# A DeltaNet and PReLU kernel: the first chunk's two steps in turn, and the first feed-forward product in halves by token

## The chip, the cores and the metric

The kernel runs on one core of a Trainium2 chip. A core has a matrix engine (TensorE, here PE, with its weight loads shown as PEld), VectorE (DVE), ScalarE (ACT), GpSimd (POOL), and SyncE (SP), which here only issues transfers. Each engine works through its own instructions in order, and semaphores tie the engines together. The metric is the device time of one execution in microseconds (us).

## The reference

Two blocks, one behind the other. The first is a DeltaNet recurrence for 4 batches, 8 heads, 768 tokens and head dimension 48; the second is a feed-forward with a learned slope for negative values, for 3072 tokens, model width 384 and inner width 2048.

```python
k_n = k / (norm(k) + 1e-6)
for t in range(768):
    y[:, :, t] = q[:, :, t] @ state
    v_old = state^T @ k_n[:, :, t]
    state = state + beta[:, :, t] * outer(k_n[:, :, t], v[:, :, t] - v_old)
x = y as (batch * token, head * dim)             # 3072 x 384
h = x @ w_in                                     # 384 x 2048
g = maximum(h, 0) + alpha * minimum(h, 0)
out = g @ w_out                                  # 2048 x 384
```

`w_in` and `w_out` arrive as float64 and are turned into float32 on the chip.

## The kernel before

**Steps.** The recurrence is worked in 12 chunks of 64 tokens. A step is one chunk of two of the four batches, so there are 24 steps, numbered so that steps 0 and 1 are chunk 0, steps 2 and 3 chunk 1. Within a step the 64 tokens' dependence on one another is a triangular system. Its two 32-token diagonal blocks are inverted on DVE for four steps together (`eliminate`, `eliminate_small`; a set of four is called m, and `turned` and `inverse` hold the result and its transpose). For the first four steps the inversion is done on 16-token blocks, and small matmuls join the halves: `cross` for steps 2 and 3, and the opening of `first_chunk` for steps 0 and 1. `place` copies the inverse blocks into `inv`; `between_1` and `between_2` compute with PE the block that joins the two 32-token halves (a product, a copy out of PSUM to `mid`, a product, a copy into `inv`). Then `solve` gives the corrected values u, `outputs` the step's y, `next_state` the state behind it, and `to_ffn` turns y round into `xt`, the feed-forward's input, of which a chunk has 256 tokens (128 from each step). For chunk 0 the state is zero, so `through_state` issues nothing. `mask` cuts the query-key products of steps 0 and 1 to the triangle, `scale_v` weights the values.

**Feed-forward.** `ffn_in(c)` computes g for chunk c: 8 pairs of 128 inner columns, each pair 2 x 3 matmuls of 256 tokens into one PSUM bank; ACT (L918) and DVE (L920) then apply the slope. It is a Python generator that yields after each matmul, so other work can be woven in: `alongside(products, pieces)` runs so many matmuls of chunk 0's product and so many parts of weight conversion.

**Weights.** `w_in` comes in 12 pieces of 512 KB (128 rows by 512 columns each, pieces 0 to 2 for the first 512 columns, and so on), each staged in one of six slots that lie in the space of `w_out`. A piece takes two ACT instructions (L225, L226, issued by `begin`) and two parts on DVE (L235, L240; `convert(n)` runs n parts). A slot's next piece is fetched (L209, on SP) when its last one has been converted. `ahead` limits how far ACT may run ahead. `w_out` follows in 16 pieces of 384 KB.

**PSUM.** There are eight banks: three pairs that `ps_big` and `ps_one` hand out in turn, and two for the feed-forward (`ps_ffn`).

**The order by hand.** The engines are scheduled manually: each runs its instructions in the order in which the Python program issues them. After the preparation of steps 0 to 3, `busy(6)` issues products that nothing uses (512 columns each), DVE inverts the 16-token blocks, and `first_chunk` begins. It does each stage for step 0 and step 1 together, with two `busy` products, the 12 parts of conversion of pieces 0 to 5 among and behind the outputs, and the loads for steps 2 to 4 (`load_late`, L161, and `load_v`, L137: 12 transfers in all) between the conversion parts. `second_pair` follows: it works steps 2 and 3 stage by stage, and between the stages runs chunk 0's `ffn_in` (48 matmuls) and 22 parts of conversion. Behind it come chunk 1's `ffn_in`, the next inversion (`eliminate(1)`) and the rest of `w_out`.

Of the kernel before, what the change touches and what calls it, by code (L numbers as in the profile page):

```python
# [28 lines left out]
ALU = mybir.AluOpType  # L29
# [14 lines left out]
def kernel(  # L44
# [36 lines left out]
    def ps_one():  # L81
        return ps_big()[:, 0]
# [494 lines left out]
    def quad(i):  # L577
        return slice(HB * i, HB * i + HB)
# [40 lines left out]

    def place(n, parts=(0, 1, 2, 3), by_vector=False):  # L620
        for _ in placing(n, parts, by_vector):
            pass

    def placing(n, parts, by_vector=False):


        if n >= N:
            return
        m, j = n // NJ, n % NJ
        own = slice(j * H, j * H + H)  # L630

        def put(cols, i):
            out, x = inv[n % NE][:, :, cols], inverse[m][:, own]
            if by_vector:
                nc.vector.tensor_scalar(
                    out=out, in0=x, scalar1=which[:, i : i + 1], scalar2=None, op0=ALU.mult
                )
            else:
                nc.scalar.mul(out, x, which[:, i : i + 1])  # L639

        if 0 in parts and n >= NJ:
            nc.scalar.copy(diag[n % NE], turned[m][:, own])
            yield
        if 1 in parts:
            put(slice(HB, C), 1)
            yield
        if 2 in parts:
            put(slice(0, HB), 0)
            yield
        if 3 in parts:  # L650
            w = stats[n][1]
            for t in range(2):
                nc.scalar.copy(w[half(1 - t), 2], w[half(t), 1])
            yield
# [19 lines left out]

    def copied(n, second, p, vector=False):

        to = inv[n % NE][:, :, HB:C] if second else mid[n % 2]
        to = to.rearrange("p (a g) i -> p a g i", a=2)

        def copies():  # L680
            for t in range(2):
                rows = quad(2 * t + (0 if second else 1))
                if vector:
                    nc.vector.tensor_copy(out=to[rows], in_=p[rows])
                else:
                    nc.scalar.copy(to[rows], p[rows])  # L686

        return [copies]

    def between(*wanted, vector=False):  # L690

        wanted = [
            (n, second, region(p, G * HB, g=G)) for n, second, p in wanted if n < N
        ]
        todo = [products(*x) for x in wanted]
        for i in range(H):
            for product in todo:
                for t in range(2):
                    product(i, t)
        return [y for x in wanted for y in copied(*x, vector)]  # L700

# [8 lines left out]

    def scale_v(n):
        if n < N and n not in nv:
            nv[n] = v_raw.pop(n)
            nc.vector.tensor_tensor(
                out=nv[n], in0=nv[n],
                in1=stats[n][0][:, :, None].to_broadcast([128, H, D]), op=ALU.mult,
            )
# [180 lines left out]

    def ffn_in(c):
        xt = xts[c]  # L900
        gs = gss[c] = []
        later = iter(())
        for f in range(0, FT, 2):
            p_h = ps_ffn().rearrange("p (f i) -> p f i", f=2)
# [23 lines left out]
        for _ in later:  # L928
            pass

    def store(c, u, o_sb):
# [431 lines left out]
    def busy(n, p=None):  # L1363

        p = ps_one() if p is None else p
        while n > 0:
# [7 lines left out]
    def queries():  # L1374
# [17 lines left out]
        return mask  # L1392

    def first_chunk(mask, convert):

        both, bs = (0, 1), 2 * H
        ahead[0] = n_in

        p = ps_one()[:, 0 : bs * LB].rearrange("p (b i) -> p b i", i=LB)
        for b in range(bs):  # L1400
            for i in range(4):
                nc.tensor.matmul(p[quad(i), b], edge[quad(i), b], turned[0][quad(i), b, 0:LB])
        nc.scalar.copy(half_way[:, 0:bs, 0:LB], p)
        begin_in(6)
        busy(0.75)
        one, two = (
            ps_one()[:, 0 : bs * LB].rearrange("p (b i) -> p b i", i=LB) for _ in range(2)
        )
        for b in range(bs):
            for i in (0, 2):  # L1410
                nc.tensor.matmul(
                    one[quad(i), b], inverse[0][quad(i), b], half_way[quad(i), b, 0:LB]
                )
        for i in (0, 2):
            y = turned[0][quad(i), 0:bs, 0:LB]
            nc.vector.tensor_tensor(out=y, in0=y, in1=one[quad(i)], op=ALU.add)
        for b in range(bs):
            for i in range(4):
                nc.tensor.matmul(
                    two[quad(i), b], half_way[quad(i), b], inverse[0][quad(i), b, LB:HB]  # L1420
                )
        scale_v(0)
        y = inverse[0][:, 0:bs, LB:HB]
        nc.vector.tensor_tensor(out=y, in0=y, in1=two, op=ALU.add)
        for i in both:
            now(between_1(i, vector=i == 1))
            place(i, (1,), True)
        place(0, (2,))
        place(1, (2,), True)
        scale_v(1)  # L1430
        for i in both:
            now(between_2(i, vector=i == 1))
        mask(0)
        for i in both:
            now(through_state(i))
            now(solve(i))
        mask(1)
        busy(0.5)
        now(outputs(0))
        state_of = [next_state(0)]  # L1440
        to_ffn(0, ps_ffn())
        now(outputs(1))
        state_of.append(next_state(1))
        convert(4)
        to_ffn(1, ps_ffn())
        convert(2)
        for i in both:
            now(state_of[i])
            load_late(i + 2)
            load_v(i + 3)  # L1450
        convert(4)
        ahead[0] = FT * DM
        convert(2)

# [85 lines left out]

    first_chunk(mask, convert)
    fetch_out(SPACES)
    assert n + 22 == PARTS_IN + 10

    first_in = ffn_in(0)
    convert_on = chain(conv_in, part(conv_out, 10))
# [4 lines left out]
    def second_pair():  # L1551
# [4 lines left out]
        squares(x)  # L1556
        alongside(4, 2)
        for h in halves:
# [4 lines left out]
        squares(x + 1)  # L1563
        alongside(5, 2)
        next(halves[0])
# [3 lines left out]
        now(weigh(x))  # L1569
        alongside(4, 2)  # L1570
        next(halves[1])
        now(weigh(x + 1))
        alongside(4, 2)
        for i in both:
            now(between_1(i))
        now(grams(x))
        squares(x + 2)
        alongside(5, 3, (chain(*(placing(i, (1, 2, 3)) for i in both)), 6))
        for i in both:
# [6 lines left out]
        now(weigh(x + 2))  # L1586
        alongside(5, 3)
        y = ps_big()
# [4 lines left out]
        squares(x + 3)  # L1593
        alongside(5, 3)
        y = ps_big()
# [7 lines left out]
        now(weigh(x + 3))  # L1603
        alongside(5, 2)
        pieces = []
# [4 lines left out]
        for i in both:  # L1610
            load_late(i + 2)
            load_v(i + 3)
        alongside(5, 2)
        for i in both:
            to_ffn(i)
        now(grams(x + 3))
        alongside(IN_PARTS - 42, 1)

# [159 lines left out]
```

## Time and profile before

| | |
|---|---|
| median of 14 runs | 670.42 us (668.53 to 672.12) |
| the profiled execution | 670.4 us |
| its span in the profile | 668.7 us |
| PE busy | 643.1 us, 9535 matmuls and as many weight loads in the records |
| PEld, DVE, ACT, POOL busy | 568.9, 492.2, 263.2, 93.1 us |
| DMA | 37.72 MB, mean 56 GB/s |

The profile counts one written float32 matmul as two weight loads and two matmuls. Times in a timeline run from the start of the span. In a timeline line, the first number is the start, the second the duration of a run of equal instructions (`x75` of them); the bracket gives the engine's idle time before it and who ended it, where "issue" means that nothing which the profile shows was waited for. In a windows line come the length, then busy time and instructions of PE, PEld, DVE, ACT and POOL, then the granted clock of PE, the DMA share and GB/s. SPq lines are issues on SP, with the time that SP spent on them.

### The profile page before, as it was taken

The page shows a single profiled execution, that of the slowest core. Times are in us where ns is not written, and L with a number is a line of the kernel's source. Part 1 is how long each engine was busy: PE and PEld are TensorE (multiplying, and loading weights), DVE is VectorE, ACT ScalarE, POOL GpSimd, SP SyncE. Part 2 cuts the span into 40 slices and gives each one's busy share as a digit, 9 for nine tenths or more (in the row PEclk, how much of TensorE's full clock was granted, in tenths as well). Part 3 has the DMA queues.
Part 4 walks back from the last instruction along what each step waited for, and adds up shares of the span by engine and source line. Part 5 has one row for each costly group of instructions (what it writes and reads, how often), then busy time and mean ns, then how long its engine had stood idle before and what let it go on. Part 6 is the DMA issues. An engine that isn't in the chain of part 4 may idle for free.

```text
span 668.7 us, 22092 instructions
## 1 busy us (share of the span) xinstructions
PE 643.1 (96%) x9535; PEld 568.9 (85%) x9535; DVE 492.2 (74%) x1180; ACT 263.2 (39%) x613; POOL 93.1 (14%) x201
## 2 busy tenths in 40 slices
PE   5978998999999999999999999999999999999997
PEld 4566887656688998998998998998999999999997
DVE  5865888877999859748959747859869658568283
ACT  5726856334445333334333333223234245042140
POOL 6000211101010100001000000000035034053260
PEclk9959899998999999999999999999999999999999
DMA  8837754211342032022122112112112210100000
GB/s 125 234 89 219 194 127 119 72 32 23 71 83 44 10 70 49 14 62 49 19 45 37 21 43 37 20 43 36 27 37 38 37 35 5 25 14 1 25 1 25
DMA packets 110962, 37.72 MB, mean 56 GB/s; under 512 B 104160, under 2 KB 107248, under 8 KB 110864
## 3 DMA queue, kind: packets, MB, share of 16 engines
q1 hardware_dynamic: 109088, 35.81, 24.8%
q8 instruction: 75, 1.23, 0.8%
q10 hardware_dynamic: 1776, 0.49, 0.4%
q14 instruction: 23, 0.19, 0.1%
HBM read 31.56 MB, written 4.72 MB: 54 GB/s over the span
## 4 chain that ended last, share of the span: by engine, by line
PE 82%; DVE 10%; ACT 3%; issue 2%; DMA 2%; SPq 1%; POOL 0%; ACTq 0%; DVEq 0%; POOLq 0%
PE p_ffn L908 21%; PE p_ffn L972 17%; PE p_more L1225 8%; PE p_more L1140 4%; PE p_ffn L1130 3%; PE p_ffn L1225 3%; PE p_pair L671 3%; PE p_pair L375 3%; PE p_ffn L1135 2%; PE p_pair L740 2%; PE p_pair L765 2%; PE p_pair L778 2%; DVE prod L514 2%; DVE block L520 2%; PE p_ffn L950 2%
## 5 line engine op out<-in xcount | busy, mean ns | idle before, releaser
L908 PE MATMUL p_ffn<-xt,w_in 128*128 128x256 f32 x768 | 176.7, 385 | 3.8 <-ACT sums L918 1.8
L908 PEld LDWEIGHTS p_ffn<-xt,w_in 128*128 128x128 f32 x768 | 143.8, 191 | 24.8 <-ACT sums L918 2.2
L920 DVE SCALAR_TENSOR_TENSOR act<-act,al_t,p_ffn 128x256 f32<-128x256 f32 x112 | 48.6, 475 | 31.0 <-ACT act L918 30.9
L918 ACT ACTIVATE act<-p_ffn 128x512 f32<-128x512 f32 x56 | 33.3, 594 | 81.2 <-PE p_ffn L908 81.0
L520 DVE TENSOR_TENSOR block<-block,prod 128x30 f32<-128x30 f32 (+9 forms) x150 | 49.9, 332 | 5.2
L1164 POOL TENSOR_TENSOR k_t<-k_t 128x128 f32<-128x128 f32 (+1 forms) x48 | 29.6, 616 | 167.4 <-ACT k_t L1159 164.9
L514 DVE TENSOR_TENSOR prod<-block 128x30 f32<-128x30 f32 (+9 forms) x150 | 48.7, 325 | 3.2 <-POOL block L504 1.6
L972 PE MATMUL p_ffn<-w_out,act 128*128 128x192 f32 x288 | 49.6, 328 | 0.1
L364 POOL TENSOR_TENSOR beta_t<-beta_t,rec 128x8 f32<-128x8 f32 x24 | 6.2, 260 | 293.7 <-DVE rec L362 256.5
L972 PEld LDWEIGHTS p_ffn<-w_out,act 128*128 128x128 f32 x288 | 46.5, 190 | 0.8 <-issue 0.5
L819 ACT COPY xt<-p_pair 128x384 f32<-128x384 f32 x22 | 10.4, 478 | 91.2 <-PE p_pair L817 77.4
L1164 POOL TENSOR_TENSOR block<-block 128x128 f32<-128x128 f32 (+1 forms) x48 | 28.0, 582 | 16.7 <-ACT block L1159 14.2
L1130 PE MATMUL p_ffn<-xt,w_in 128*128 128x256 f32 x96 | 28.7, 381 | 0.5 <-DVE o_sb L992 0.5
L686 ACT COPY inv<-p_pair 32x256 f32<-32x256 f32 x46 | 16.6, 362 | 26.8 <-DVE u L769 23.6
L750 DVE TENSOR_TENSOR r<-v_raw,p_pair 64x192 f32<-64x192 f32 (+1 forms) x66 | 23.3, 353 | 1.8 <-PE p_pair L740 0.7
L769 DVE TENSOR_TENSOR u<-p_pair,wgt 128x384 f32<-128x384 f32 x24 | 13.2, 555 | 15.4 <-PE p_pair L671 14.8
L1179 DVE SCALAR_TENSOR_TENSOR act<-block,al_t,act 128x256 f32<-128x256 f32 x32 | 19.1, 638 | 5.1 <-ACT block L1175 5.1
L992 DVE TENSOR_TENSOR o_sb<-u,p_ffn 128x192 f32<-128x192 f32 x24 | 7.9, 350 | 20.2 <-PE p_ffn L972 19.7
L639 ACT ACTIVATE inv<-inverse,which 128x256 f32<-128x256 f32 x45 | 22.0, 504 | 1.8 <-DVE inverse L487 1.4
L1225 PE MATMUL p_more<-w_out,act 128*128 128x192 f32 x128 | 21.9, 329 | 0.0
L1159 ACT COPY k_t<-p_more 128x512 f32<-128x512 f32 x16 | 9.4, 586 | 31.4 <-PE p_more L1140 26.7
L729 ACT COPY y<-p_pair 128x384 f32<-128x384 f32 x22 | 10.4, 479 | 28.6 <-PE p_pair L725 26.6
(223 smaller groups left out, 1408.9 us busy)
## 6 DMA issues: line engine op xcount, KB each, us to landing
w_out<-in_moe_w_in_dram SPq DMA_DIRECT2D x12, 512.0 KB, 5.8
qp<-in_q_dram SPq DMA_DIRECT2D x48, 96.0 KB, 3.1
v_raw<-in_v_dram SPq DMA_DIRECT2D x48, 96.0 KB, 3.1
kl<-in_k_dram SPq DMA_DIRECT2D x96, 48.0 KB, 2.8
out_dram<-o_sb SPq DMA_DIRECT2D x92, 48.0 KB, 1.6
space_out<-in_moe_w_out_dram SPq DMA_DIRECT2D x11, 384.0 KB, 3.8
ke<-in_k_dram SPq DMA_DIRECT2D x43, 96.0 KB, 3.3
w_out<-in_moe_w_out_dram SPq DMA_DIRECT2D x5, 384.0 KB, 4.8
```

The lines of the kernel that those rows point to most:

```text
L514: nc.vector.tensor_tensor(out=prod, in0=r[:, 0:j, j : j + 1].to_broadcast([128, j, n]), in1=r[:, j : j + 1, j + 1 : HB].to_broadcast([128, ...
L520: nc.vector.tensor_tensor(out=r[:, 0:j, j + 1 : HB], in0=r[:, 0:j, j + 1 : HB], in1=prod, op=ALU.add)
L639: nc.scalar.mul(out, x, which[:, i : i + 1])
L750: nc.vector.tensor_tensor(out=r[to, a], in0=v_in[to, a], in1=p[own, a, :, 0:D], op=ALU.subtract)
L908: nc.tensor.matmul(p_h[:, i], w_in[:, t, (f + i) * 128 : (f + i + 1) * 128], xt[:, t], start=(t == 0), stop=(t == KT - 1),)
L918: nc.scalar.activation(g, p_h, ACT.Relu, scale=-1.0)
L920: nc.vector.scalar_tensor_tensor(out=g[:, i], in0=g[:, i], scalar=al_t[:, f + i : f + i + 1], in1=p_h[:, i], op0=ALU.mult, op1=ALU.add,)
L972: nc.tensor.matmul(p, x(i), w(i), start=(i == 0), stop=(i == FP - 1))
L1130: nc.tensor.matmul(p[:, f * 256 : f * 256 + 256], w(2, f), xt[:, 2], start=True, stop=False)
L1140: nc.tensor.matmul(q[:, j], a, b, start=True, stop=True)
L1164: nc.gpsimd.tensor_tensor(out=dst, in0=a, in1=b, op=ALU.add)
L1225: nc.tensor.matmul(p, x(i), w(i), start=(i == 0), stop=(i == FP - 1))
```

## The change

`first_chunk` no longer does its stages for both steps together. The opening is written as a generator `crossing(i)` for one step. Both steps' first part is issued, then step 0 goes alone through its second part, `place`, `between_1`, `between_2`, `solve`, `outputs` and `to_ffn`, with six `busy` products (five of 384 columns, one of 128) between the stages instead of two. Conversion parts stand between these stages; step 1's second part follows, and step 1's stages then alternate with matmuls of chunk 0's `ffn_in`. All 12 parts of conversion now stand before the loads for steps 2 to 4.

For this, the first four pairs of chunk 0's `ffn_in` are written by `ffn_in_split`: all 24 products for step 0's 128 tokens first, then the 24 for step 1's. The four pairs keep four PSUM banks meanwhile: one pair of `big`, so two remain to be handed out in turn, and the two feed-forward banks. The evacuations follow in step 1's half. The first half is issued in `first_chunk`, the second at the beginning of `second_pair`; the other four pairs come in `ffn_in(c, 8)` as before. `alongside` in `second_pair` has other numbers of products and parts, with the same sums (24 halves and 24 whole products, 22 parts).

Two of the placings of `inv` and the scaling of step 1's values go from DVE and ACT to POOL, the other two placings to ACT. Of step 1's copies, one of two goes to DVE, not both. `begin_in(7)` starts piece 6 on ACT ahead of step 1's `to_ffn`. `busy` writes to the bank that is handed out next, without taking it out of turn.

```diff
+    def ffn_in_split(c, pairs):
+        xt = xts[c].rearrange("p k (u b e) -> p k b u e", u=2, b=2)
+        gs = gss[c] = []
+        own = big.pop(0)
+        p_h = [own[:, 0], own[:, 1]] + [ps_ffn() for _ in range(pairs - 2)]
...
+        for b in range(2):
+            for j in range(pairs):
+                p = p_h[j].rearrange("p (f u b e) -> p f b u e", f=2, u=2, b=2)
+                for i in range(2):
+                    for t in range(KT):
+                        f = 2 * j + i
...
+                        nc.tensor.matmul(
+                            p[:, i, b], w_in[:, t, f * 128 : f * 128 + 128], xt[:, t, b],
+                            start=(t == 0), stop=(t == KT - 1),
+                        )
+                        if (i, t) != (1, KT - 1):
+                            yield
+                if b == 1 and j == 1:
+                    evacuated(0)
+                if b == 1 and j > 0:
+                    evacuated(j)
+                yield
+            if b == 1:
+                big.append(own)
+        yield from ffn_in(c, 2 * pairs)
...
     def first_chunk(mask, convert):
+        halves = [crossing(i) for i in range(2)]
+        for h in halves:
+            next(h)
         begin_in(6)
         busy(0.75)
+        next(halves[0])
+        busy(0.75)
+        place(0, (1,))
+        now(between_1(0))
+        place(0, (2,), True)
+        scale_v(1, nc.gpsimd)
+        convert(2)
         scale_v(0)
+        busy(0.75)
+        now(between_2(0))
+        mask(0)
+        mask(1)
+        busy(0.75)
+        now(through_state(0))
+        now(solve(0))
+        convert(1)
+        busy(0.75)
+        now(outputs(0))
+        convert(3)
+        busy(0.25)
+        to_ffn(0, ps_one())
+        next(halves[1])
+        first_in = ffn_in_split(0, 4)
...
+        place(1, (1,))
+        place(1, (2,), True)
+        ffn(4)
+        convert(2)
+        now(between_1(1, both=True))
+        ffn(4)
+        convert(2)
+        now(between_2(1, both=True))
+        ffn(4)
+        convert(2)
+        now(through_state(1))
+        now(solve(1))
+        ffn(4)
+        now(outputs(1))
+        ffn(4)
+        begin_in(7)
+        to_ffn(1, ps_one())
+        ffn(2)
+        now(next_state(0))
+        ffn(2)
+        now(next_state(1))
+        for i in range(2):
             load_late(i + 2)
             load_v(i + 3)
-        convert(4)
         ahead[0] = FT * DM
-        convert(2)
+        return first_in
...
     def second_pair():
         squares(x)
-        alongside(4, 2)
+        alongside(7, 1)
         for h in halves:
             next(h)
         flips(x, n)
...
         squares(x + 1)
-        alongside(5, 2)
+        alongside(7, 1)
         next(halves[0])
         flips(x + 1, n + 1)
...
-        alongside(4, 2)
+        alongside(7, 2)
         next(halves[1])
         now(weigh(x + 1))
-        alongside(4, 2)
+        alongside(3, 2)
         for i in both:
             now(between_1(i))
         now(grams(x))
         squares(x + 2)
-        alongside(5, 3, (chain(*(placing(i, (1, 2, 3)) for i in both)), 6))
+        alongside(4, 3, (chain(*(placing(i, (1, 2, 3)) for i in both)), 6))
```

The later calls of `alongside` become (4, 3), (4, 3), (4, 3), (4, 2) and (4, 2).

## The prediction

> **What bounds the kernel now.** I read the page first: the 40 slices, then the DMA queues.
>
> ```profile
> PE   5978998999999999999999999999999999999997
> ...
> PEclk9959899998999999999999999999999999999999
> DMA  8837754211342032022122112112112210100000
> ...
> q8 instruction: 75, 1.23, 0.8%
> ```
>
> A slice is 16.7 us. After the first 120 us PE is busy without a break and at full clock, so the change, which reorders work between 27 and 95 us, pays only in what PE loses there; what it wins there moves everything behind it forward, and as much is won at the end. Queue q8 is needed below: 1.23 MB over PE's 2 x 9535 instructions is 64 bytes each, so it brings PE's program, 256 instructions a packet. I call these pages. A written matmul is two weight loads and two matmuls, so a page holds 64 written matmuls, however small.
>
> PE's timeline from 26 us on, kept to the lines with idle time before them and one slow run:
>
> ```profile
> 33.20 1.20 PE L1419 MATMUL p_pair<-inverse,act 32*32 32x16 f32 x75 [1.55 <-issue]
> ...
> 37.76 0.58 PE L671 MATMUL p_pair<-turned,right 32*32 32x32 f32 x15 [2.17 <-issue]
> ...
> 49.64 1.99 PE L908 MATMUL p_ffn<-xt,w_in 128*128 128x256 f32 x8 [0.57 <-ACT xt L819]
> ...
> 67.12 0.91 PE L671 MATMUL p_pair<-turned,right 32*32 32x32 f32 x32 [3.21 <-DVE turned L615]
> 68.59 4.11 PE L908 MATMUL p_ffn<-xt,w_in 128*128 128x256 f32 x10
> ```
>
> Two losses say "issue" and stand inside runs of equal matmuls. The windows between them explain it:
>
> ```profile
> 33.20:37.76 4.56, 2.38 (x129) 2.29 (x129) 0.77 (x2) 1.24 (x3) 0.00 (x0) 0.50 0.59 109
> 37.76:42.07 4.31, 3.66 (x126) 3.47 (x125) 2.95 (x8) 0.72 (x2) 0.00 (x0) 0.50 0.02 4
> ```
>
> From stall to stall run 129 matmuls and 129 weight loads: one page. The DMA view shows one q8 packet in each such window. Counting pages of 256 on from 33.20, PE enters one at 28.66, 33.20, 37.76, 42.07, 47.72, 52.56, 57.00 and 61.07. The shortest distances are 4.07 to 4.84 us: tiny matmuls go no faster than 64 per page, and a page takes longer while DMA is loaded (the column before the last is GB/s). The column after POOL is the clock: 0.50 throughout the first chunk.
>
> Last, the chain of waits, and SP's timeline for its origin:
>
> ```profile
> 58.14 5.29 DMA w_out<-in_moe_w_in_dram
> 63.45 0.68 ACT w_in L225
> 64.14 0.65 ACT w_out L226
> 64.80 0.49 ACT act L918
> 65.31 0.87 DVE act L920 x2
> 66.18 0.60 DVE w_in L240
> 66.78 0.20 DVE turned L615
> ```
>
> ```profile
> 45.48 2.45 SPq L209 DMA_DIRECT2D w_out<-in_moe_w_in_dram  x3
> 48.03 3.50 SPq L161 DMA_DIRECT2D kl<-in_k_dram  x4
> 51.58 1.29 SPq L137 DMA_DIRECT2D v_raw<-in_v_dram  x2
> 52.96 3.72 SPq L161 DMA_DIRECT2D kl<-in_k_dram  x4
> 56.73 1.29 SPq L137 DMA_DIRECT2D v_raw<-in_v_dram  x2
> 58.14 2.57 SPq L209 DMA_DIRECT2D w_out<-in_moe_w_in_dram  x3
> ```
>
> The last three pieces of w_in are issued behind 12 small loads that stand ahead of them in SP's order. ACT stops in order for the first of them until 63.45, and with it the evacuation, the `turned` addition and PE (3.21 us). The ten matmuls at 68.59 take 4.11 us; at 0.224 us each (24 in 5.38 us at 115.2) they are 2.24. So 3.2 + 1.9 = 5.1 us stall.
>
> **The change, part by part.** I take written matmuls from the start of `first_chunk` as the measure. The stall at 33.20 is 64 + 1 + 32 + 21.5 = 118.5 into it; pages begin at 54.5, 118.5, 182.5 and so on. Before, `first_chunk` is 328 of them and `second_pair` 526. The change adds 24 products of half width and 4 `busy` to the first: 356.
>
> *Conversions and fetches.* The same 12 conversion parts now begin right after step 0's `between_1`. DVE needs 1.1 us a piece (0.42 + 0.69). Piece 6 can be issued when SP ends its earlier loads at 35.04 (32.39 + 2.65), the rest follow the conversions to about 47, all ahead of the 12 small loads. A piece lands 5.8 us after issue, so the last by 53; before, it was after 63. The 5.1 us stall goes. The small loads still begin near 50, when `next_state` frees their buffers, as before at 48.03; step 2's state needs them only at 87. They cost nothing while that 25 us cover lasts.
>
> *Half-width products.* 24 products of 128 columns in the first chunk, 24 in `second_pair`, for 24 of 256. A run of four 128-column matmuls with a weight load each (L1135, at 560.21) takes 0.44 us, the two 256-column ones before it 0.44: half the columns, half the time, and loads hidden. The split costs 24 more instruction quadruples and 0 us of array time. The first 24 are 24 x 0.22 = 5.4 us of work done earlier.
>
> *Step 0's chain.* Up to 118.5 count and traffic are unchanged, so its page still comes at 33.2. From there: between_1 0.4, copy 0.75, between_2 0.5, copy 0.75, solve 0.6, u 0.55, outputs 0.6, y 0.48, with some 0.15 between them: page 182.5 is entered, in `to_ffn(0)`, at 39.0. The `busy` products lie in these waits.
>
> *Step 1's chain and 24 products.* By durations alone: crossing 1.2, the wait for xt 0.4, products 5.4, between_1 and between_2 1.0, solve 0.6, outputs 0.6, to_ffn 0.4, two next_state 1.0 and some 1.2 of copies not covered, 11.8, so 50.8. But pages bound them: 39.0 to the next three at 4.84 each (the row 47.72 to 52.56, when w_in pieces flowed) is 43.9, 48.7, 53.5. Matmul 374.5 thus begins at 53.5; by durations, with 7 products (1.6) and 11 tiny ones (0.3) more, it would be 52.7.
>
> *`second_pair`.* 8.2 pages. Matmuls 374.5 to 502.5 are mostly tiny or half width: two pages at 4.44 (the row 52.56 to 57.00, small loads flowing): 62.3. The next meets three w_out pieces (issued at 60.75 before). There the page entered at 61.07 saw its successor's packet start only at 64.89, land 0.96 later, and 1.39 more to use: 6.2. I take 5.5 as between, 67.8. The point behind `grams(x)` follows 1.0 later at 68.8; before it was 68.6. But then 24 of 48 products are done, not 17: 7 x 0.448 = 3.1 us ahead, and the 1.9 us stall behind it is gone. 3.1 + 1.9 - 0.2 = 4.8. The next page boundary takes 0.3 and one bank pair fewer 0.5 (below): 4.0 us gained.
>
> *PSUM and POOL.* Until the split ends one of three double banks is held, so `grams(x)` shares a bank with `between_1` and waits for its copy, 0.75 us: 0.5 taken. Two placings and one scaling go to POOL. No such operation is in the trace; between a 0.46 us copy (L471) and 1.2 us (1.5 x 0.78, L1164 with 256 columns) each has about 4 us until `solve` needs it: 0. If POOL took over 4 us, the excess would go into the chain.
>
> *`begin_in(7)`* holds ACT for 1.35 us ahead of xt's copy for step 1. PE has `next_state(0)` and four products then (1.4 us): 0, or 0.5 if piece 6 were late.
>
> **Weighing rules.** The trace shows page stalls of 1.55 and 2.17 us. The Trainium skill, "Runtime: NRT & Kernel Launch", section "Instruction fetch mechanics", has the same 16 KiB blocks of 256 but calls the crossing "mostly hidden"; by that the sum would be the one by durations alone in the rivals, and the rows speak against it.
>
> The clock fell to 0.50 from 31 to 48 us (0.65 in 30:34, 0.72 in 46:50) with PE seldom idle but on tiny tiles. The skill's "TensorE: Matmul & The Clock Gate", Part 1, lets a busy window of 3.4 us restore it; by that `busy` and the new products would wake PE at 34.6 or 38.0. While pages bound the stage either clock leaves the sum as it is; if not, each 3.4 us at half rate costs 1.7.
>
> **Rivals.** *Pages come freely (662).* At 4.07 (57.00 to 61.07) matmul 566.5 is reached 0.8 + 2 x 0.37 + 1.43 = 3.0 us sooner and the 0.3 vanishes: 7.3 gained, 663.1. By durations alone, `second_pair` takes 50.8 + 24 x 0.22 + 24 x 0.448 + 18.9 (from 49.64 to 95.2, the end of the six products that begin at 92.48; less 21.5 of products and 5.1 of stalls) = 85.8 instead of 95.2: 9.4 gained, 661.0. For it: quiet rows. Against: w_in now flows just where DMA was idle (4 GB/s in 37.76:42.07).
>
> *A wait for a wait (670).* In the first 200 matmuls of `second_pair` (24 x 0.22 + 160 x 0.025 + two flips of 0.9 = 11.1 us) ACT has three conversions of 1.35, four evacuations of 0.6, two double flips' copies of 1.2, squares 1.0 and small ones 1.2: 11.1; if a conversion ends late there, PE waits for `turned` as before and the gain is eaten. Against: pages stretch that stage to 15 us anyway, and its pieces landed long before.
>
> *Slower: instruction pages queue behind w_in (673).* The place is 39 to 68 us. At 6.2 us for six pages instead of 4.84 (three), 4.44 (two) and 5.5, 4.1 + 3.5 + 0.7 = 8.3 us go, so up to 4.3 us lost; I put 2.5. It decides from 0.67 us more a page, a mean of 5.5. For it: 64.89, and 22.6, where a packet started 3.1 us after its page at 400 GB/s. Against: the six pieces are spread over 12 us by the conversions, not queued at once.
>
> **How the numbers follow.** The profiled execution is 670.4 (span 668.7 and 1.7 around it), the median of 14 is 670.42, so no correction. 670.4 - 4.0 = 666.4; since several taken values lean to the dear side I say 666.0. Chances: this 0.60, free pages 0.14, a wait for a wait 0.10, slower 0.16. Within 0.2% (1.3 us) is about what a measurement here cannot tell from no change. Faster 0.74, same 0.10, slower 0.16. The range reaches from durations alone, 661.0, into the slower case, 672.0.
>
> **What would show it.** Right: no ACT wait for w_in near 58 to 63; six w_in issues on SP before the `kl` loads; between 39 and 68 us "issue" waits on PE at multiples of 129 matmuls; half-width products first near 40.5; the point behind `grams(x)` near 69 and the last product of `second_pair` near 91 (95.2 now). Wrong: PE waiting on DVE or ACT there rather than on pages, pages beyond 5.5 us, or the lead gone again between 95 and 150 us, where DVE's elimination runs beside PE.

## The result, and the profile after

| | before | after |
|---|---|---|
| median | 670.76 us (48 runs, 667.64 to 672.96) | 678.92 us (10 runs, 673.47 to 681.04) |
| ratio, 95% interval | | 1.0113 (1.0095 to 1.0130) |
| profiled execution, its span | 670.4, 668.7 us | 673.47, 671.7 us |

Slower by 8.2 us, where the sum of the prediction had a gain of 4.0. The executions of the changed kernel fall into two kinds. Of 15 with their clock on record (11 here, one more than the median counts, and four of its repetition `after_again`), three have a mean granted clock of 0.985 and take 673.5 to 674.0 us; twelve lie at 0.969 to 0.979 and take 678.0 to 681.0. The profile after is of the first kind, that of `after_again` (679.75 us, span 678.0) of the second, so there is a trace of each. (The printed ratios leave out executions over 1.5% above the fastest of their kernel; where that removes half-clock executions, I give counts.)

The 40 slices of after:

```profile
PE   5899798999999999999999999999999999999997
...
PEclk9889799998999999999999999999999999999999
DMA  8865665301341132032022022022112210100000
...
q8 instruction: 75, 1.23, 0.8%
```

The empty slices of DMA around 40 us are filled as intended, PE's slices hardly differ, and no more program is fetched. SP's timeline of after shows the fetches in their new place, six pieces of `w_in` ahead of the `kl` loads:

```profile
35.49 13.96 SPq L209 DMA_DIRECT2D w_out<-in_moe_w_in_dram  x6
52.91 2.65 SPq L161 DMA_DIRECT2D kl<-in_k_dram  x4
```

No wait of ACT for `w_in` is left near 60 us. PE's timeline of after (start, length, idle time before it):

```profile
31.34 1.65 PE L1407 MATMUL p_pair<-k_t,ident 112*128 112x384 f32 x2
...
41.76 0.55 PE L817 MATMUL p_pair<-ident,y 128*128 128x128 f32 x3 [0.18 <-ACT y L783]
...
43.40 1.16 PE L955 MATMUL p_pair<-xt,w_in 128*128 128x128 f32 x8
...
54.09 1.83 PE L955 MATMUL p_pair<-xt,w_in 128*128 128x128 f32 x14
...
67.81 0.42 PE L671 MATMUL p_pair<-turned,right 32*32 32x32 f32 x7 [0.92 <-DVE inverse L617]
69.89 0.86 PE L671 MATMUL p_pair<-turned,right 32*32 32x32 f32 x25 [1.66 <-issue]
...
71.73 3.27 PE L908 MATMUL p_ffn<-xt,w_in 128*128 128x256 f32 x8
...
101.17 2.83 PE L908 MATMUL p_ffn<-xt,w_in 128*128 128x256 f32 x12 [1.15 <-DVE act L920]
```

Between 28 and 64 us PE has no wait over 0.2 us: the page stalls and copy waits of before are gone, and PE's own speed sets the stage. ("Busy" is what the profile counts as such; a busy PE need not be at its peak.) What that speed was is in the windows, first of after, then of `after_again` (the number after POOL is the clock):

```profile
35.00:40.00 5.00, 5.00 (x69) 2.88 (x68) 1.26 (x4) 0.72 (x2) 0.00 (x0) 0.50 0.56 152
40.00:45.00 5.00, 4.82 (x173) 3.78 (x172) 3.79 (x9) 1.47 (x3) 1.02 (x1) 0.98 0.58 170
50.00:55.00 5.00, 5.00 (x122) 4.60 (x114) 1.21 (x3) 3.76 (x7) 0.00 (x0) 1.00 0.51 175
```

```profile
35.00:40.00 5.00, 5.00 (x72) 2.72 (x70) 2.01 (x5) 1.45 (x4) 0.27 (x1) 0.50 0.59 151
40.00:45.00 5.00, 5.00 (x77) 3.24 (x71) 2.62 (x5) 0.65 (x2) 0.00 (x0) 0.50 0.28 83
50.00:55.00 5.00, 5.00 (x64) 4.49 (x67) 3.09 (x6) 0.39 (x2) 0.00 (x0) 0.50 0.60 188
```

In after the half rate ends at 40.2, in `after_again` at 56.7, though PE is busy for all of these 5.00 us. The same eight instructions then take 2.08 instead of 1.16, and `second_pair` begins 7.4 us later (61.54 for 54.09), in `after_again`:

```profile
46.55 2.08 PE L955 MATMUL p_pair<-xt,w_in 128*128 128x128 f32 x8
...
61.54 1.83 PE L955 MATMUL p_pair<-xt,w_in 128*128 128x128 f32 x14
```

How far each execution is ahead of the profiled one of before, in equal work, can be read at four points. At the start of `second_pair` before has 49.64, and 24 halves (5.4 us) still to do, so 55.0; behind `grams(x)` 68.59, and the others have 7 products more (3.1 us) done; the last product of `second_pair` ends at 95.2; the run of 12 after the common wait for `sums` starts at 102.77.

| ahead of before, us | second_pair begins | behind grams(x) | last product | behind sums | span |
|---|---|---|---|---|---|
| after (clock 0.985) | 55.0 - 54.09 = 0.9 | 3.1 + 68.59 - 71.73 = 0.0 | 95.2 - 96.8 = -1.6 | 102.77 - 105.84 = -3.1 | -3.0 |
| after_again (0.975) | -6.5 | -7.1 | -8.7 | -10.1 | -9.3 |
| after_cover8 (0.992, below) | 3.6 | 2.1 | 0.6 | -0.9 | -0.1 |

Two losses are to be explained: some 7 us in the first chunk, which come and go with the clock, and 3.6 to 4.5 us given back behind it, up to the common wait for `sums`, in every row.

### The profile page after: what moved, and what is told of

The parts are those of the page before. It is cut to its first block, busy times and chain, and to the rows that moved or that the text cites. A ratio compares the mean times of both kernels' runs of the same rounds, so it can differ in the third digit from the quotient of the medians.

```text
span 671.7 us, 22202 instructions
## 1 busy us (share of the span) xinstructions
PE 646.1 (96%) x9591; PEld 571.4 (85%) x9591; DVE 493.0 (73%) x1177; ACT 264.5 (39%) x617; POOL 96.1 (14%) x204
## 4 chain that ended last, share of the span: by engine, by line
PE 79%; DVE 12%; ACT 4%; issue 2%; DMA 1%; SPq 0%; POOL 0%; DVEq 0%; POOLq 0%
PE p_ffn L908 19%; PE p_ffn L1011 17%; PE p_more L1264 8%; PE p_more L1179 4%; PE p_ffn L1169 3%; PE p_ffn L1264 3%; PE p_pair L671 3%; PE p_pair L375 3%; PE p_ffn L1174 2%; PE p_pair L740 2%; PE p_pair L765 2%; PE p_pair L778 2%; PE p_pair L422 2%; DVE block L520 2%; DVE prod L514 2%
## 5 line engine op out<-in xcount | busy, mean ns | idle before, releaser
L908 PE MATMUL p_ffn<-xt,w_in 128*128 128x256 f32 x720 | 165.4, 384 | 3.8 <-ACT sums L918 1.8
L908 PEld LDWEIGHTS p_ffn<-xt,w_in 128*128 128x128 f32 x720 | 134.7, 191 | 23.6 <-issue 2.7
L920 DVE SCALAR_TENSOR_TENSOR act<-act,al_t,p_ffn 128x256 f32<-128x256 f32 x104 | 45.1, 474 | 24.5 <-ACT act L918 24.4
L918 ACT ACTIVATE act<-p_ffn 128x512 f32<-128x512 f32 x52 | 31.0, 595 | 77.6 <-PE p_ffn L908 77.5
L1169 PE MATMUL p_ffn<-xt,w_in 128*128 128x256 f32 x96 | 28.7, 381 | 0.5 <-DVE o_sb L1031 0.5
L750 DVE TENSOR_TENSOR r<-v_raw,p_pair 64x192 f32<-64x192 f32 (+1 forms) x66 | 23.3, 353 | 1.4 <-PE p_pair L740 0.3
L1218 DVE SCALAR_TENSOR_TENSOR act<-block,al_t,act 128x256 f32<-128x256 f32 x32 | 19.7, 657 | 5.3 <-ACT block L1214 5.2
L802 DVE TENSOR_TENSOR beside<-beside,p_pair 48x384 f32<-48x384 f32 (+1 forms) x36 | 19.8, 549 | 4.3 <-ACT ksq L345 3.5
L347 DVE TENSOR_REDUCE norm<-ksq 128x8 f32<-128x384 f32 x24 | 12.9, 543 | 13.2 <-ACT ksq L345 13.2
L729 ACT COPY y<-p_pair 128x384 f32<-128x384 f32 x22 | 10.4, 479 | 29.9 <-PE p_pair L725 27.9
```

The lines of the kernel that those rows point to most:

```text
L750: nc.vector.tensor_tensor(out=r[to, a], in0=v_in[to, a], in1=p[own, a, :, 0:D], op=ALU.subtract)
L908: nc.tensor.matmul(p_h[:, i], w_in[:, t, (f + i) * 128 : (f + i + 1) * 128], xt[:, t], start=(t == 0), stop=(t == KT - 1),)
L918: nc.scalar.activation(g, p_h, ACT.Relu, scale=-1.0)
L920: nc.vector.scalar_tensor_tensor(out=g[:, i], in0=g[:, i], scalar=al_t[:, f + i : f + i + 1], in1=p_h[:, i], op0=ALU.mult, op1=ALU.add,)
L1169: nc.tensor.matmul(p[:, f * 256 : f * 256 + 256], w(2, f), xt[:, 2], start=True, stop=False)
```

## The experiments

**Theory:** the change makes PE the bound of a stage that runs at half clock, so it pays for the clock; the rest of the lead goes to waits in `second_pair`. **Rivals:** the halves and the bank that they hold cost it; instruction pages behind `w_in`; the serial order itself.

### The parts of the change

**early_fetch, early_fetch_5** (before, with all conversion parts ahead of the small loads):

```diff
         for i in both:
             now(state_of[i])
-            load_late(i + 2)
-            load_v(i + 3)
         convert(4)
         ahead[0] = FT * DM
         convert(2)
+        for i in both:
+            load_late(i + 2)
+            load_v(i + 3)
```

> One part alone, in the kernel before: all 12 conversion parts ahead of the 12 small loads, so w_in's last three pieces are issued ahead of them on SP. If the 5.1 us stall at 63 to 72 us is a net loss, as the prediction has it: 666 us, and ACT's wait for w_in is gone. If ACT and VectorE set these stages as soon as the wait is gone: 668.5 to 670.

> early_fetch again with more rounds: a version that may beat both kernels. From the first look (667.6 to 669.3 on the same chip): a ratio of 0.997 to 0.999. If the removed wait for w_in is worth its 5 us: 0.993.

Measured: 667.63 us for 669.3, ratio 0.9987 (0.9963 to 1.0011); in five rounds 670.11 for 670.04, 0.9999 (0.9980 to 1.0018). ACT's wait for `w_in` near 60 us (3.51 us in before) and PE's behind it are gone in both profiles, but in `early_fetch_5` a page comes late instead: the page that PE entered at 52.24 saw its successor's packet start only at 55.7, and

```profile
57.99 0.42 PE L608 MATMUL p_pair<-inverse,act 32*32 32x16 f32 x26 [1.11 <-issue]
```

It reaches the point behind `grams(x)` at 67.60, 1.0 us before before. In the profile of `early_fetch`, the fastest of its executions, that wait is 0.28 us; there the point comes at 63.55, 5.0 us before before, of which 1.9 stood already at the first whole product (47.72 for 49.64), and the span is 664.1. So a single execution can keep the gain, but the medians do not: the stall, costed at 5.1 us, is worth at most 1.3 us by the five rounds and 2.5 by the three (the lower ends of the intervals).

**split_only** (before's order, the first four pairs of `ffn_in(0)` as halves of 128 columns, each with its own weight load; arguments shortened to `...`):

```diff
-                    nc.tensor.matmul(p_h[:, i], w_in[...], xt[:, t], ...)
+                    if c == 0 and f < 8:
+                        for b, k_ in order[2 * t : 2 * t + 2]:
+                            nc.tensor.matmul(p[:, b], w_in[:, k_, ...], x[:, b], ...)
```

> The kernel before, its order kept, with the first four pairs of chunk 0's product written as halves of 128 columns by step, each weight loaded twice. The prediction had halves at no cost in array time: 670. In the changed kernel's trace a run of 14 half matmuls takes 1.75 us instead of 1.54: by that 96 half matmuls cost 1.2 to 1.5 us, 671; with a page of instructions more on top 672.

671.23 for 670.81, 1.0012 (0.9995 to 1.0029): not told from nothing. By the trace of after a half's instruction takes 0.125 to 0.135 us (14 in 1.75, 54.09 to 55.84; 8 in 1.08, 43.40 to 44.48) and not 0.112, so the 96 cost 1.2 to 2.2 us of array time; how much of it lies in waits is not shown.

**serial_order** (after, without the halves: step 0 and step 1 one behind the other, six `busy`, `ffn_in(0)` whole in `second_pair` with before's numbers) and **serial_twobusy** (the same with the two `busy` of before):

```diff
-        first_in = ffn_in_split(0, 4)
...
-        ffn(4)                  # and the other calls of ffn
-        return first_in
+        return ffn_in(0)
...
-        alongside(7, 1)
+        alongside(4, 2)         # and the others as before
```

> The change without its products: step 0 ahead of step 1, with the same six products that nothing uses, the early conversions and the POOL instructions, but chunk 0's ffn_in whole and unsplit, all of it in second_pair with the numbers of before. Clock theory (the change fills PE in a stage at half rate, so PE's rate becomes the bound): the 12 us that 24 halves take there at half rate are gone, 5.4 us come back at full rate, so some 5 us under the change's usual 678.7: 672 to 674, and the time depends less on the clock. If the order by steps itself is the loss: as the change, 677 or more. If the products were the only loss: 668, as early_fetch.

> serial_order with two products that nothing uses, as before (384 and 256 columns), not six. Four products at half rate of 1.3 us each leave PE's order of step 0. If PE's rate at half clock bounds step 0's chain: 2 to 4 us faster than serial_order. If copies and pages bound it: the same within 1 us.

674.76 for 670.04 (1.0076, 1.0053 to 1.0100), and 673.85 (1.0057, 1.0036 to 1.0078). The order alone costs some 4 us in the median. A likely reason, not tested by itself, is that each step's short products and copies follow each other, where before did them for two steps at once. The first whole product begins at 53.64 in the trace of `serial_twobusy` (half rate from 29.9 to 57.3), at 50.75 in that of `serial_order` (43.3 to 53.5 in this stage; its best execution, 670.01 us at a mean clock of 0.984, where the other four have 0.977 and 674.1 to 675.3) and at 49.64 in before (31.2 to 48.3), so part of these 4 us is the clock again. The halves have to win this back before they bring anything.

**two_pairs** (after_longbusy, below, with two pairs as halves: 12 halves in the first chunk, no bank held):

```diff
-        own = big.pop(0)
-        p_h = [own[:, 0], own[:, 1]] + [ps_ffn() for _ in range(pairs - 2)]
+        p_h = [ps_ffn() for _ in range(pairs)]
...
-        first_in = ffn_in_split(0, 4)
+        first_in = ffn_in_split(0, 2)
```

> after_longbusy (672.4, of which six of eight executions near 671.8) with two pairs of the product in halves instead of four: 12 halves in the first chunk, 12 in second_pair with 36 whole ones, and all three double banks in turn. If the bank that is held costs the waits at 63.6, 66.9 and 76.8 us of the changed kernel's trace: 2 us faster, 670, though 2.7 us of products move behind the first chunk. If these waits come from the order on ACT and VectorE: 673 to 674.

677.18, 1.0096 (1.0061 to 1.0131); at clocks 0.987 and above three executions of 675.9 to 678.0. Giving the bank back does not help. What the bank costs by itself is not shown, since this version also does 12 halves fewer in the first chunk. Without the bank PE waits for an evacuation instead, in PE's timeline of `two_pairs`:

```profile
59.77 2.05 PE L908 MATMUL p_ffn<-xt,w_in 128*128 128x256 f32 x4 [2.53 <-DVE act L941]
```

### The clock

**after_again** is the changed kernel once more, for a second trace (no edit).

> The changed kernel once more, unchanged, for a profile of one of its longer executions (the profiled one took 673.5 us, eight of ten 678 to 681). Clock theory: an execution of about 679 us shows some 15 us more at a granted clock of 0.50 than the profiled one (20 us), and it lies between 27 and 75 us. Page theory: the clock is alike, and PE's idle time put down to issue between 39 and 68 us is 5 us more.

678.66 us, 1.0115 (1.0076 to 1.0155); its trace is read above. It has 34.1 us at half rate against 20.4 in after, and in neither does PE wait for "issue" between 39 and 68 us, so the clock theory came and the page theory did not.

**after_nobusy** (after without its six `busy`), **after_longbusy** and **longbusy_again** (the first of them 2.0 long for 0.75), **after_busy3** (3.0):

```diff
         begin_in(6)
-        busy(0.75)
+        busy(2.0)               # after_busy3: busy(3.0)
```

> The changed kernel without the six products in first_chunk that nothing uses. If at half rate they stretch step 0's chain (1.65 us each where the copies take less) and do not restore the clock: 2 to 3 us faster than the change, to_ffn(0) near 39.0 instead of 41.8. If they are what restores the clock in some executions: slower, 680 us or more, with the clock at 0.50 until the first products of the feed-forward have run.

> The changed kernel with the first of these six products longer (2 x 512 columns and none of 384), so that PE works on full tiles for some 1 us more in the window in which the clock falls. Clock theory: the clock stays at 1.00 from 27 to 60 us in most executions, and the time falls to 670 to 674. Page theory: as the change, or 1 us slower.

> after_longbusy again for a profile of one of its usual executions (six of eight: clock 0.98 to 0.995, 671 to 672.7). Clock theory: granted clock 1.00 from 27 to 60 us, and first_chunk's last next_state ends near 52 instead of 61 us (54 in the change's shorter execution). What is left between it and the kernel before stands as PE's idle time between 55 and 80 us.

> The changed kernel with its first unused product four times as long (3.0 for 0.75; 2.5 us more array time at full clock, 5.0 at half). So far executions whose mean granted clock was 0.985 and above took 670.7 to 674 us, those at 0.982 and below 676 to 685; with 0.75 two of some 14 were of the first kind, with 2.0 eleven of 16. Theory (the half granted clock makes the difference, and a longer run of full products at the front ends it early): with 3.0 nearly all executions at 0.985 and above, their time 671.5 to 673.5 (up to 1.1 us of the added products not covered by the copy beside it), at most one in five above 676. Rival (the clock only accompanies a difference that has another cause, a fetch or the order): the two kinds stay mixed as with 2.0, or the median goes up to 676 and above by the added products, at whatever clock.

| first busy | executions at clock 0.985 and above | their time | the others |
|---|---|---|---|
| none of six | 0 of 4 | | 674.2 to 678.4 us |
| 0.75 | 3 of 15 | 673.5 to 674.0 us | 678.0 to 681.0 us |
| 2.0 | 10 of 16 | 670.7 to 673.2 us | 676.0 to 685.0 us |
| 3.0 | 12 of 12 | 670.6 to 673.8 us | none |

(The shares "two of some 14" and "eleven of 16" in the expectation of `after_busy3` were miscounts; the runs have 3 of 15 and 10 of 16.) With 2.0 the medians are 672.4 and 672.0 us (1.0051, 1.0028 to 1.0074, and 1.0044, 1.0005 to 1.0082). More unused work on PE's path makes the kernel faster, by a fuller clock: with 3.0 the ratio is 1.0033 (1.0018 to 1.0048), for 1.9 us more of products (2.84 us for 0.91 in the traces; the expectation had 2.5). That is the clock theory's side; the rival's 676 and above did not come. Without the six the median is 676.75 us, 1.0107 (1.0079 to 1.0134), 1.9 us under `after_again` measured beside it, its profile at half rate from 30.5 to 51.0: less work at half clock, and the clock no better.

**before_longbusy**, **fetch_longbusy** (the same edit on before and on early_fetch) and **before_hold** (before with the first `busy` 3.0 long and three more of 0.75 in its chain):

```diff
             place(i, (1,), True)
+            busy(0.75)
...
             now(between_2(i, vector=i == 1))
+        busy(0.75)
```

> The kernel before with its first product that nothing uses in first_chunk made longer (2 x 512 columns and none of 384). Before, the clock is at 0.50 for 17 us from 31 us on. If half rate in the first chunk costs time in this order too: clock near 0.99, 666 to 668. If this order is bound there by instruction pages and copies, not by the array's rate: 670 to 671, the added 1 us of products in the path.

> The same longer product in the kernel before with the 12 conversion parts ahead of the small loads (early_fetch, 667.6 alone). If both gains add: 664 to 666. If the one takes what the other would: 667 to 668.

> The kernel before with more unused products: the first 3.0 long instead of 0.75, and one of 0.75 behind each of the two between_1 with its place and one behind both between_2; 5 us more array time at full clock, nearly all of it in waits for copies. It asks what the half rate costs the order of before. Theory (the order of before waits for pages and copies in the first chunk, so PE's rate is worth little to it): whatever the clock, 669 to 674, not under the kernel before by over 1 us. Rival (half rate costs both orders alike, some 3 us for 17 us of it): where the clock comes out at 0.99 and above, 666 to 668.5.

671.31 for 670.81 (1.0017, 0.9992 to 1.0043), 669.94 (0.9996, 0.9964 to 1.0027) and 672.69 for 670.61 (1.0041, 1.0017 to 1.0066). Before gains nothing by such products, even where `before_hold` has a clock of 0.992: 670.5 to 671.4 us in three executions, not the rival's 666 to 668.5. (`before_longbusy` and `fetch_longbusy` do not test this: their clocks are 0.975 to 0.989, as in before.) This does not make before wholly indifferent: among 120 executions of it beside these runs, the 32 at 0.984 and above take 669.2 us in the mean and the 12 below 0.978 671.6. It is some 2 us over its range of clocks, against 4 to 8 between the two kinds of the changed kernel.

**after_cover8**, **before_cover8** (eight unused products for six ahead of the inversion, where PE stood idle):

```diff
-    busy(BUSY)                  # BUSY = 6
+    busy(8)
     begin_in(5)
     for _ in eliminate_small(0):
```

> The changed kernel with busy(8) instead of busy(6) ahead of the inversion; nothing else. In executions in which those six products ran at full clock PE then stands idle for 2.3 to 3.0 us before the first chunk, and the granted clock drops at 29.4 to 30.0; two products more take 1.8 us at full clock and fill most of that gap. Theory A (the idle time ahead of the first chunk sets off the half rate): most executions come at clock 0.985 and above and take 671 to 674. Theory B (the tiny products, 32 x 32 tiles, of the opening set it off, whatever is ahead): the clock stays at 0.970 to 0.979 in most executions and the time is 677 to 681, up to 1.8 more where the eight products end after what they wait beside.

> The kernel before with busy(8) instead of busy(6). Theory (its first chunk waits for pages and copies at either clock): 669 to 672.5, whatever the clock. Rival (half rate costs it as it does the changed kernel): below 668 in executions at 0.99 and above.

This pair decides. `after_cover8` takes 671.47 us for 670.11, 1.0021 (0.9998 to 1.0044), ten of 12 executions at 0.985 and above; `before_cover8` 670.31, 1.0001 (0.9978 to 1.0024). Two products that nothing uses, far ahead of everything that the change touched, take back 6.8 of its 8.2 us (1.4 us over the kernel before in place of 8.2, each against the runs of before beside it), and are worth nothing to before. There they do not move the clock either (0.980 to 0.985, within before's range), so what a full clock is worth to before rests on `before_hold` alone. In PE's timeline of `after_cover8` the gap ahead of the first chunk (2.3 us in after, 3.0 in `after_again`) is closed:

```profile
19.56 8.97 PE L1407 MATMUL p_pair<-k_t,ident 112*128 112x512 f32 x16
28.46 1.59 PE L1445 MATMUL p_pair<-turned,sums 32*32 32x16 f32 x128
...
51.41 1.83 PE L955 MATMUL p_pair<-xt,w_in 128*128 128x128 f32 x14
...
65.12 0.31 PE L671 MATMUL p_pair<-turned,right 32*32 32x32 f32 x3 [0.90 <-DVE inverse L617]
67.60 0.96 PE L671 MATMUL p_pair<-turned,right 32*32 32x32 f32 x29 [2.17 <-issue]
...
69.55 3.78 PE L908 MATMUL p_ffn<-xt,w_in 128*128 128x256 f32 x8
```

The clock stays full from 23.3 to 64.3 us, through all tiny products of the opening, so theory B of the expectation falls, and `second_pair` begins 3.6 us ahead of before. This trace alone does not show that the two products closed the gap: its eight ran at half rate until 23.3 (their instructions start 0.85 us apart, then 0.43), and where the clock rises earlier eight leave a gap of 0.54 (`cover8_lead5`) or 0.64 us (`before_cover8`). The argument rests on the ten of 12 executions. Then the lines from 65.12 on give it back.

### What is left at full clock

**cover8_lead5** (after_cover8 with five whole products more ahead of the two `between_1`) and **cover8_lead5_short** (the same, and the five `busy` of 384 columns cut to 256):

```diff
-        alongside(3, 2)
+        alongside(8, 2)         # 1 + 2 + 2 products fewer in the last three calls
...
-        busy(0.75)
+        busy(0.5)               # five times, in cover8_lead5_short alone
```

> after_cover8 with five whole products more in front of the two between_1 of second_pair (8 instead of 3), taken from the last four calls of alongside. At full clock they are 1.1 us and lie where PE waits 0.9 us for DVE's inverse addition (at 64.2 in after_cover8) and 2.2 us for a page (at 65.4). Theory (second_pair loses the lead to waits of PE and the half rate that follows them): the first wait goes, the second shrinks, and the time falls by 1 to 2.5 us to 669 to 670.5. Rival (the stages behind are set by ACT, DVE and pages, and products taken from them leave waits there): the same as after_cover8 within 1 us.

> cover8_lead5 with the five unused products of 384 columns in step 0's chain cut to 256. In after_cover8 step 0's chain has no wait of PE over 0.3 us, so each of these products is as long as the copy that it covers or longer; five times 0.3 us of array time less. Theory (step 0's chain is set by PE): 0.5 to 1.5 us less than cover8_lead5. Rival (copies set it, or less work lets the clock drop again): the same or, with clocks at 0.98 and below, 675 and more.

Both theories failed, and in the second run the rival's drop of the clock came. `cover8_lead5` takes 676.98 us (1.0105, 1.0087 to 1.0122), `cover8_lead5_short` 682.76 (1.0196, 1.0175 to 1.0218). Five products are ten instructions, 2.2 us and not the 1.1 expected, and their weights are not there yet, as PE's timeline of `cover8_lead5` shows:

```profile
69.65 1.56 PE L908 MATMUL p_ffn<-xt,w_in 128*128 128x256 f32 x6 [1.88 <-DVE w_in L240]
```

So the filler for those waits is limited by DVE's conversions: the waits of 0.90 and 2.17 us are gone, and this one of 1.88 has come. Where the products were taken away waits grew too, as the rival had it (ahead of L375 1.39 us for 0.19, for `sums` 2.30 for 1.84); these do not add up to the whole loss, and the rest is not explained. And some 1.0 us of products less in step 0's chain (five times 0.70 for 0.91 us at full clock) made the kernel 5.8 us slower: all five executions of the short version are at 0.972 to 0.975, its profile at half rate from 29.8 to 57.1. In `cover8_lead5` itself the clock is not the main reason: its one execution at 0.992 took 675.4.

## Why the prediction was wrong, step by step

Of the 12.2 us between the sum (4.0 faster) and the result (8.2 slower), 6.8 go with the clock by `after_cover8`; the other 5.4 are left at full clock, and are lost between the start of `second_pair` and the common wait for `sums`.

**The step that failed: "While pages bound the stage either clock leaves the sum as it is."** It put the half clock at nothing, and pages do not bound the changed first chunk. Counted as the prediction counts, after enters pages at 41.81 and 44.86, 3.05 us apart, nearer than the 4.07 of before, and this while DMA moved 252 GB/s. The rows that gave the prices of a page were no limits of pages either: PE was busy for 4.44 of 4.44 and 4.07 of 4.07 us in them, so they time PE's own work. First three windows of before, then one of after:

```profile
47.72:52.56 4.84, 4.20 (x139) 3.33 (x136) 3.95 (x9) 2.74 (x6) 0.00 (x0) 0.94 0.91 285
52.56:57.00 4.44, 4.44 (x127) 3.87 (x128) 2.37 (x5) 4.38 (x10) 0.00 (x0) 1.00 0.70 109
57.00:61.07 4.07, 4.07 (x144) 3.53 (x137) 2.73 (x8) 1.77 (x5) 0.47 (x2) 1.00 0.57 91
```

```profile
41.81:44.86 3.05, 3.05 (x129) 2.73 (x129) 1.90 (x6) 0.99 (x2) 0.88 (x1) 1.00 0.86 252
```

With halves and `busy` in every wait it is PE's rate that counts, and the rate was half for 10.2 us in the trace of after (the kind of three of 15 executions) and for 27.3 in that of `after_again` (the kind of the others). That is 6.3 us between the two spans. The rule "each 3.4 us at half rate costs 1.7" stood in the prediction as the other case and had no rival with a price; by it the 17.1 us more at half rate cost 8.5, and the two traces are 7.4 apart at the start of `second_pair`.

The other terms of the sum:

- **"The `busy` products lie in these waits"**: at half clock one takes 1.65 us (31.34, 33.91, 36.49) for copies of 0.75. `to_ffn(0)` came at 41.76 rather than 39.0 in the better trace, at 43.89 in the other. In `after_cover8`, at 0.91 each, it came at 39.14, from an opening 0.9 us later than in before.
- **The stall of 5.1 us**: it vanished as described (no ACT wait, six issues early) but by `early_fetch_5` is worth at most 1.3 us. Its second term, 1.9 us, was no wait: the clock of before falls to 0.50 from 68.7 to 72.2, just under the ten products, and in after from 67.5 to 74.3, under the line at 71.73 (3.27 for 1.8). Instructions at half rate beside a wait were read as part of the wait. The first term came back as page and DVE waits (0.92 and 1.66 us at 67.81 and 69.89).
- **The stage up to `grams(x)`, and the lead**: the sum had 15.3 us for it (53.5 to 68.8). It took 17.6 in after, 17.3 in `after_again` and 18.1 in `after_cover8`, so it was sized too small at either clock. In `after_cover8` the first chunk is ahead of the forecast (51.41 for 53.5), and the lead of 3.6 us is reached; 4.5 us of it are lost again by 103 us. There stand the waits of 0.45, 0.90 and 2.17 us (before had one of 3.21), a half-rate stretch of 10.2 us for 3.4 (64.3 to 74.5), and one new wait of 1.15 us for DVE's evacuation (`act` L920). No run removes one of these alone, so how they share the loss is not shown. The prediction named the loss "between 95 and 150 us" as a sign of error; it begins at 61.
- **Halves at no cost**: 1.2 to 2.2 us of array time.
- **The serial order**: costed as a chain with "1.2 of copies not covered"; by the two serial runs it costs some 4 us against both steps together, the clock's share included. This was missing from the sum, but at full clock the first chunk came in under the sum all the same.
- **Right**: POOL's operations (1.03 us for a placing, 0.82 for the scaling) and `begin_in(7)` cost nothing; the fetches' new order; no page wait from 39 to 64 us, so the slower rival, pages queued behind `w_in`, was not the reason either, though `early_fetch_5` shows that such a delay occurs. The chance of 0.16 for a slower kernel stood for that reason, not for the one that came.

A rule decided here. The Trainium skill, "TensorE: Matmul & The Clock Gate", Part 1, has the clock back at full after about 3.4 us of busy PE. The prediction weighed it and set it aside as harmless. In the runs it did not hold for this work: `after_again` has PE busy, as the profile counts it, without a wait over 0.2 us from 29.4 to 56.7 us, eight times that length, at 0.50. What the clock counts as busy no run shows.

What stays open: that the clock makes the two kinds of executions rests on the two kinds in one and the same program and on four edits of filler alone that shift both together (first `busy` 2.0 and 3.0, eight for six, and the shorter ones). What makes the clock return at 40.2 in one execution and at 56.7 in another of the same program is not settled. Nor is the gap ahead of the first chunk the only trigger: before's clock falls at 31.2 with no such gap, and in `cover8_lead5` at 30.1 behind one of 0.54 us. No version was faster than before clear of noise.

## What to carry to other kernels

Before filling an engine's waits with useful work, ask what rate the engine has in that stage: waits hide a half clock, and an order that removes them pays for it. Put the granted clock beside equal instructions that take longer than elsewhere, before calling it a stall. And where an early stage is made of tiny products, filler that nothing uses, placed in an idle stretch ahead, can be worth several times its length; price it by trying one longer and one shorter, and count executions rather than read one trace.

## What the runs showed of the hardware

- A PE that the profile shows busy throughout did not restore the clock: 0.50 for 27.3 us in `after_again`, with PE busy for 5.00 of each 5.00 us. Changes of the granted clock lie multiples of 3.4 us apart (half rate for 10.2 us in after, 27.3 in `after_again`, 17.1 in before, 3.4 in `longbusy_again`).
- The clock reacts to little: 1.8 us of products more ahead of the stage took 6.8 us away, some 1.0 us fewer inside it added 5.8.
- The six products ahead of the inversion take 7.65 us in before's trace and 5.42 in after's, as the clock rises later or earlier under them (24.4 and 19.7 us). The later it rises, the smaller the gap behind them. Behind a late rise no half rate followed in the first chunk of `after_cover8` (23.3) and `after_busy3` (24.3), but one did in before (31.2); whether an early half rate prevents a later one is open.
- A loaded DMA does not by itself hold a page to the 4.07 to 4.84 us that the prediction read from its rows: one took 3.05 us at 252 GB/s in after. But a packet can start late: in `early_fetch_5` 3.5 us behind the entry of its page (52.24 to 55.7), against 1.8 in before (52.56 to 54.39).
